# Eighteen small products ahead of the first scores, and part of the value loads asked for later

## The chip, the cores and the metric

One core of one Trainium2 chip. The metric is the device time of one execution in microseconds; the median over several executions is compared. Engines are named TensorE (matmuls, PE in the rows, with PEld for its weight loads), VectorE (DVE), ScalarE (ACT), GpSimd (POOL) and SyncE (SP), which issues nearly all transfers.

## What is computed

Strided attention, then a gated product with two matrices behind it, then a mixture of four experts. Everything is float32 in and out.

```python
# attention: batch 2, 8 heads, 576 positions, head size 64
scores = q @ k.T / 8                      # per head
mask_local   = (rel >= 0) & (rel < 32)    # heads 0 to 3
mask_strided = (rel >= 0) & (pos_k % 32 == pos_q % 32)   # heads 4 to 7
attn = softmax(where(mask, scores, -1e9)) # sum + 1e-9 in the denominator
x = (attn @ v)                            # to 1152 tokens x 512
# gated product
h = ((x @ w1) * (x @ w2)) @ w3            # 512 -> 1024 -> 1024
x = h @ w_out                             # 1024 -> 512
# experts
p = domain_probs / (sum(domain_probs) + 1e-9)
out = sum over e of p[:, e] * (relu(x @ w1[e]) @ w2[e])
```

## The kernel before

The order of all instructions is written out by hand, under one schedule from line 823 on; each engine does its instructions in that order. Four stages follow each other: attention of the first batch (lines 824 to 973), the first products of the weights w1 and w2 with the first batch's x, into which the second batch's attention is woven (974 to 1029), the small product of w3 and w_out (1030 to 1053), and the experts (1055 to 1126).

**Attention.** `warm_up` (107) makes a zeroed tile `idle` and sends products of it through TensorE that nobody reads; `keep_warm(n, parts)` sends n more of them, 128 columns for each part. One float32 product of this program appears in the trace as two weight loads and two matmuls. The batch has six chunks (`Chunk4`): three for the local heads (g = 0) and three for the strided heads (g = 1). A chunk goes through `masks` and `scores` (TensorE), `maxima` and `subtract` (VectorE), `exps` (ScalarE), the reciprocal of the sums (`sums`, or `slots_exps` and `recip` for chunk 1, VectorE), `normalise` (GpSimd, chunk 5 VectorE), `transposes` (TensorE), `evac` (ScalarE), `pv`, the product with the values (TensorE, line 483 for local and 492 for strided heads), and `put`, which stores the result in `x_whole` (ScalarE, line 521).

**Loads.** SyncE issues its transfers in program order, and the kernel's transfers rotate through eight semaphores. The values of the local heads come by `load_v_loc(b, c, behind)`, one load or three to a chunk; with `behind` given, GpSimd first copies a column of that tile into the target (328), so the transfer cannot be issued before the tile is written. `load_v_str` and `load_v_rest` bring the values of the strided heads, 54 = T3 partitions to a piece. In the kernel before, line 917 holds the second chunk's load behind the first chunk's maxima, and the third chunk's, the strided values and the rest follow it directly.

**Weights.** w1, w2, w_out and w3 arrive as 64-bit floats in chunks of 1 MB and are turned into float32 by integer steps: `round_up` (or `whole_low`) and `magnitude` on ScalarE, `clamp`, `shift`, `sign` and `add` (or `whole_steps`) on VectorE. Then each is split into a high part (`split_hi`, ScalarE) and a low part (`split_lo`, VectorE), and a product is three products, high by high, high by low and low by high (`mm3`, 301). The first chunk (`zero`, c_w12[0]) comes in two halves by `whole_load` (941) behind a GpSimd memset, is not split, and is multiplied with `x_whole` by `whole_product` (585) at lines 974 to 1002. The second (`one`) follows at lines 983 to 1007. From the third (`two`, c_w12[2]) on the steps run in the generator `work` (258), one step for each `advance`. At most two raw chunks wait in `rawp`, apart from three that borrow another place.

**Around the change**, TensorE's order is: warm-up, masks and scores 0, 1, 2, `keep_warm`, scores 3, transposes 0, scores 4, transposes 1, scores 5, pv 0, transposes 2, pv 1, transposes 3, pv 2, pv 3, transposes 4, `keep_warm(1, 2)`, transposes 5, pv 4, pv 5, then the whole products.

Of the kernel before, what the change touches and what calls it, by code (L numbers as in the profile page):

```python
# [8 lines left out]
F32 = mybir.dt.float32  # L9
# [5 lines left out]
ALU = mybir.AluOpType  # L15
# [3 lines left out]
P = 128  # L19
W = 32  # L20
# [4 lines left out]
T3 = 3 * NB  # L25
# [3 lines left out]
NBLK = NT // BLK  # L29
NTT = NT // P  # L30
NEG = -8.0e9
WARM = 2
SCALE = 1.0 / float(D) ** 0.5

EXP_LO, EXP_HI = 3.0517578125e-05, 122880.0
# [7 lines left out]
def kernel(  # L43
# [63 lines left out]
    def warm_up():  # L107

        idle = tmp.tile([P, P], F32, tag="pT", name="idle")
        nc.vector.memset(idle, 0.0)  # L110
        nc.scalar.activation(small.tile([P, 1], F32, tag="rec", name="one"), idle[:, :1], AF.Exp)
        moving = idle.unsqueeze(1).to_broadcast([P, 4, P])

        def keep_warm(n, parts=4):
            if n:
                acc = bank("idle").rearrange("p (a b) -> p a b", a=4)[:, :parts]
            for i in range(n):
                mm(acc, idle, moving[:, :parts], start=i == 0, stop=i == n - 1)

        keep_warm(WARM)  # L120
        return keep_warm


# [4 lines left out]
    class Chunk:  # L128
# [78 lines left out]
        def add_halves(self):  # L207
# [3 lines left out]
            for i in range(2):  # L211
                c = slice(512 * i, 512 * i + 512)
                self.add_half(i)
                nc.scalar.copy(self.hi[:, c], self.f32[:, c])

        def low_halves(self):
            for c in (slice(0, 512), slice(512, 1024)):
                nc.vector.tensor_tensor(out=self.lo[:, c], in0=self.f32[:, c], in1=self.hi[:, c].bitcast(F32),
                                        op=ALU.subtract)
            self.done = True  # L220

        def split_half(self, i, src):
            if i == 0:
# [26 lines left out]
    def load_next(held=False):  # L250
        nonlocal loaded
        if loaded < len(stream):
            stream[loaded].raw_load(held)
            loaded += 1
            for load in rest_loads.pop(loaded, ()):
                load()

    def work():


        wide = stream[2:20]
        before = None
        for c, after in zip(wide, wide[1:] + [None]):
            if before:
                while live > 14:
                    yield False
                before.split_hi()
            c.clamp()
            yield True
            if before:  # L270
                before.split_lo()
            c.shift()
            yield True
            c.sign()
            yield True
            if after:
                after.round_up()
                after.magnitude()
            c.add()
            yield True  # L280
            before = c
        while live > 14:
            yield False
        before.split_hi()
        yield True
        before.split_lo()
        yield True
        for w in c_e:
            yield from w.work()
# [11 lines left out]
    def mm3(acc, lhs, rhs, first, last):  # L301
        (lh, ll), (rh, rl) = lhs, rhs
        mm(acc, lh, rh, start=first, stop=False)  # L303
        mm(acc, lh, rl, start=False, stop=False)  # L304
        mm(acc, ll, rh, start=False, stop=last)  # L305


    x_hi = xp.tile([P, 4, NT], F32R, tag="x_hi", name="x_hi")
    x_lo = xp.tile([P, 4, NT], F32R, tag="x_lo", name="x_lo")
# [36 lines left out]
    def load_v_str(b):  # L346

        tv = big[0].tile([P, 12, P], F32, tag="big", name="tv_str")
        row = 5 * P
        for k in range(2):  # L350
            at = v_str[b, k, 0, 0]
            rows = bass.AP(tensor=at.tensor, offset=at.offset, ap=[[row, T3], [T3 * row, 2], [1, row]])
            nc.sync.dma_start(out=tv[64 * k:64 * k + T3, :10].rearrange("p (h t) d -> p h (t d)", h=2), in_=rows)
        vals[b, 1] = tv

    def load_v_rest(b):
        for k in range(2):
            nc.sync.dma_start(out=vals[b, 1][64 * k:64 * k + NB, 10:], in_=v_str[b, k, 2 * T3:2 * T3 + NB, :2])

    class Chunk4:  # L360
# [104 lines left out]
        def evac(self, copy):  # L465
            n = self.frames * P
            self.pT = tmp.tile([P, 512], F32, tag="pT", name="pT")[:, :n]
            copy(self.pT, self.tp)
# [81 lines left out]
    def ab_block(b, ft, n):  # L550
# [16 lines left out]
            hi, lo = (x[b, pair][:, ft % 2, n * HB:n * HB + HB] for x in (ab_hi, ab_lo))  # L567
        for w in range(2):
            acc = bank("ab_acc")[:, :HB]
            for k in range(4):  # L570
                mm3(acc, c_w12[ft].parts((w * 4 + k) * P, P), (x_hi[:, k, t], x_lo[:, k, t]), k == 0, k == 3)
            if w == 0:
                nc.scalar.copy(ab, acc)  # L573
            else:
                nc.vector.tensor_tensor(out=full, in0=acc, in1=ab, op=ALU.mult)
            yield
# [246 lines left out]
    with tc.manual_schedule():  # L823
# [91 lines left out]
        first[1].scores()  # L915
        first[0].maxima()
        load_v_loc(0, 1, first[0].mx[:, :1])
        load_v_loc(0, 2)
        load_v_str(0)
        load_v_rest(0)  # L920
        first[0].subtract()
        first[0].exps()
        first[2].scores()
# [7 lines left out]
        first[4].scores()  # L931
        exp_of(2)
        first[1].recip()
        first[1].normalise()
        evac(0)
        first[1].transposes()
        first[5].scores()
# [20 lines left out]
        scale_of(5)  # L958
        load_qk(1, 0, held=True)
        load_next()  # L960
        zero.whole_low(0)
        put(2)
        first[4].transposes()
        evac(4)
        zero.whole_low(1)
        keep_warm(1, 2)
        first[5].transposes()
        zero.whole_steps(0)
        first[4].pv()
        evac(5)  # L970
        put(3)
        put(4)
        first[5].pv()
        firsts = [ps_sc.tile([P, 512], F32, tag="sc", name="ab_acc")[:, :HB], bank("ab_acc")[:, :HB]]
# [214 lines left out]
```

## Time and profile before

| | us |
|---|---|
| median of 3 runs | 618.88 (617.59 to 619.91) |
| the profiled execution | 622.39 |
| its span, first to last instruction | 620.6 |
| TensorE busy | 611.4 (99%) |
| VectorE busy | 442.4 (71%) |
| ScalarE busy | 279.6 (45%) |
| GpSimd busy | 9.1 (1%) |
| mean granted clock of TensorE | 0.994 |

Times in the rows are counted from the first instruction of the span. Busy shares are means over the whole span, and the stages differ: attention of the first batch fills about the first 28 us. A matmul's end is modelled, so TensorE counts as busy while matmuls overlap; that it stood is read from the idle time in brackets and from the chain.

### The profile page before, as it was taken

What the parts mean: (1) busy time and instruction counts of PE and PEld (TensorE: products, weight loads), DVE (VectorE), ACT (ScalarE), POOL (GpSimd) and SP (SyncE); (2) the same over time, 40 slices, a digit from 0 to 9 for tenths busy, and PEclk for the clock granted to TensorE, in tenths of its full rate; (3) what the DMA queues carried; (4) which work ended last, traced back from release to release, by engine and by line L of the source; (5) the groups of instructions that cost most, each with busy time, mean ns of one, the idle gap of its engine ahead of it and who ended that gap; (6) DMA issues with size and microseconds to landing.
All of it is one profiled execution on the core that took longest, in us unless ns stands there. A gap on an engine that the chain in (4) does not pass through costs nothing.

```text
span 620.6 us, 11293 instructions
## 1 busy us (share of the span) xinstructions
PE 611.4 (99%) x4584; PEld 558.0 (90%) x4584; DVE 442.4 (71%) x796; ACT 279.6 (45%) x555; POOL 9.1 (1%) x33
## 2 busy tenths in 40 slices
PE   8799999999999999999999999999999999999998
PEld 5689999998889999999889999899989898989997
DVE  4699996988774126777876987888776665755843
ACT  4678974666643224433443334343433333333320
POOL 4100000000000000000000000000000000000000
PEclk9799999999999999999999999999999999999999
DMA  8967251244532111343354353445586556465411
GB/s 254 350 241 224 72 173 45 69 135 143 203 131 85 53 69 32 132 176 137 137 202 149 129 199 137 158 181 170 187 314 229 197 211 227 181 219 189 142 62 69
DMA packets 28403, 99.44 MB, mean 160 GB/s; under 512 B 2632, under 2 KB 6288, under 8 KB 25920
## 3 DMA queue, kind: packets, MB, share of 16 engines
q1 hardware_dynamic: 28080, 98.43, 45.1%
q8 instruction: 36, 0.59, 0.4%
q10 hardware_dynamic: 272, 0.29, 0.1%
q14 instruction: 15, 0.12, 0.1%
HBM read 79.58 MB, written 19.14 MB: 159 GB/s over the span
## 4 chain that ended last, share of the span: by engine, by line
PE 86%; DVE 5%; ACT 3%; DMA 3%; issue 2%; SPq 0%; DVEq 0%
PE g_acc L303 11%; PE g_acc L304 11%; PE g_acc L305 11%; PE m_a L305 4%; PE m_a L304 4%; PE m_a L303 4%; PE m_b L304 3%; PE m_c L303 3%; PE x_acc L305 3%; PE x_acc L303 3%; PE x_acc L304 3%; PE m_c L304 3%; PE m_b L303 3%; PE m_c L305 3%; PE m_b L305 3%; PE wc_acc L303 2%
## 5 line engine op out<-in xcount | busy, mean ns | idle before, releaser
L732 ACT ACTIVATE h_hi<-u 128x320 fp32r<-128x320 f32 (+1 forms) x128 | 56.9, 445 | 189.2 <-DVE u L738 189.2
L303 PE MATMUL g_acc<-w_hi,h_hi 128*128 128x512 f32 (+1 forms) x296 | 114.3, 386 | 0.0
L304 PE MATMUL g_acc<-w_lo,h_hi 128*128 128x512 f32 (+1 forms) x296 | 114.2, 386 | 0.0
L305 PE MATMUL g_acc<-w_hi,h_lo 128*128 128x512 f32 (+1 forms) x296 | 113.7, 384 | 0.0
L671 DVE TENSOR_TENSOR w_lo<-raw,w_hi 128x768 fp32r<-128x768 f32 x64 | 69.4, 1085 | 12.5 <-ACT w_hi L669 12.4
L738 DVE TENSOR_TENSOR u<-m_b,u 128x320 f32<-128x320 f32 (+1 forms) x96 | 40.8, 452 | 50.8 <-PE m_b L305 50.8
L303 PE MATMUL ab_acc<-x_hi,w_hi 128*128 128x288 f32 x240 | 71.7, 299 | 0.4 <-ACT ab L573 0.3
L304 PE MATMUL ab_acc<-x_lo,w_hi 128*128 128x288 f32 x240 | 70.7, 294 | 0.0
L305 PE MATMUL ab_acc<-x_hi,w_lo 128*128 128x288 f32 x240 | 70.7, 294 | 0.0
L305 PEld LDWEIGHTS g_acc<-w_hi,h_lo 128*128 128x128 f32 x296 | 55.6, 188 | 11.6
L303 PEld LDWEIGHTS g_acc<-w_hi,h_hi 128*128 128x128 f32 x296 | 55.8, 188 | 8.0
L304 PEld LDWEIGHTS g_acc<-w_lo,h_hi 128*128 128x128 f32 x296 | 55.7, 188 | 7.6
L734 DVE SCALAR_TENSOR_TENSOR h_lo<-u,h_hi 128x320 fp32r<-128x320 f32 (+1 forms) x128 | 57.7, 451 | 3.7 <-ACT h_hi L732 1.9
L669 ACT CAST w_hi<-raw 128x768 fp32r<-128x768 f32 x64 | 60.0, 937 | 0.0
L303 PEld LDWEIGHTS ab_acc<-x_hi,w_hi 128*128 128x128 f32 x240 | 45.0, 188 | 1.0 <-ACT ab L573 0.5
L304 PEld LDWEIGHTS ab_acc<-x_lo,w_hi 128*128 128x128 f32 x240 | 45.0, 188 | 0.0
L305 PEld LDWEIGHTS ab_acc<-x_hi,w_lo 128*128 128x128 f32 x240 | 45.0, 188 | 0.0
L304 PE MATMUL m_b<-b_t,s_hi 128*128 128x320 f32 (+1 forms) x128 | 37.9, 296 | 0.0
L738 DVE TENSOR_TENSOR u<-m_a,u 128x320 f32<-128x320 f32 (+1 forms) x64 | 28.9, 452 | 11.6 <-PE m_a L305 11.6
L671 DVE TENSOR_TENSOR s_lo<-raw,s_hi 128x1024 fp32r<-128x1024 f32 x16 | 19.6, 1226 | 24.3 <-ACT s_hi L669 24.3
L738 DVE TENSOR_TENSOR u<-m_c,u 128x320 f32<-128x320 f32 (+1 forms) x64 | 29.0, 453 | 4.5 <-PE m_c L305 3.9
L748 ACT COPY u<-m_a 128x320 f32<-128x320 f32 (+1 forms) x32 | 12.8, 400 | 42.1 <-PE m_a L305 42.1
(178 smaller groups left out, 1416.7 us busy)
## 6 DMA issues: line engine op xcount, KB each, us to landing
raw<-in_e_dram SPq DMA_DIRECT2D x32, 1024.0 KB, 5.2
raw<-in_w3T_dram SPq DMA_DIRECT2D x8, 1024.0 KB, 5.0
stored<-s_hi SPq DMA_DIRECT2D x16, 512.0 KB, 2.6
stored<-s_lo SPq DMA_DIRECT2D x16, 512.0 KB, 2.7
s_hi<-stored SPq DMA_DIRECT2D x16, 512.0 KB, 4.7
s_lo<-stored SPq DMA_DIRECT2D x16, 512.0 KB, 5.6
raw<-in_w_dram SPq DMA_DIRECT2D x7, 1024.0 KB, 6.5
raw<-in_w_out_dram SPq DMA_DIRECT2D x4, 1024.0 KB, 4.9
```

Source lines behind the costliest of these rows:

```text
L303: mm(acc, lh, rh, start=first, stop=False)
L304: mm(acc, lh, rl, start=False, stop=False)
L305: mm(acc, ll, rh, start=False, stop=last)
L669: nc.scalar.copy(dst[0], src)
L671: nc.vector.tensor_tensor(out=dst[1], in0=src, in1=dst[0].bitcast(F32), op=ALU.subtract)
L732: nc.scalar.activation(hi, src, AF.Relu)
L734: nc.vector.scalar_tensor_tensor(out=lo, in0=src, scalar=0.0, in1=hi.bitcast(F32), op0=ALU.max, op1=ALU.subtract)
L738: nc.vector.tensor_tensor(out=out, in0=acc, in1=b, op=ALU.add)
L748: nc.scalar.copy(u1, a)
```

## The change

The warm-up's second product of 512 columns becomes one of 256, and ahead of it come 18 products of a 64 x 64 piece of the zeroed tile with 32 columns. The third chunk's local values are held behind chunk 1's reciprocal, the strided values and the rest come behind chunk 1's `normalise` in program order, and the strided values are read for 64 partitions instead of 54. On ScalarE `put(2)` now stands ahead of `whole_low(0)`, and `whole_low(1)` between `put(3)` and `put(4)`. The third weight chunk is added and split by halves in `work`, and its first product runs all products with the high weights ahead of those with the low ones.

```diff
-        keep_warm(WARM)
+        keep_warm(1)
+        acc = bank("idle")
+        for i in range(FILL):
+            r = slice(64 * (i % 2), 64 * (i % 2) + 64)
+            mm(acc[r, :W], idle[r, :64], idle[r, :W], start=True, stop=True)
+        keep_warm(1, 2)
...
+        def low_half(self, i):
+            c = slice(512 * i, 512 * i + 512)
+            nc.vector.tensor_tensor(out=self.lo[:, c], in0=self.f32[:, c], in1=self.hi[:, c].bitcast(F32),
+                                    op=ALU.subtract)
+            self.done = i == 1
...
-            if before:
+            first_wide = before is wide[0]
+            if before and not first_wide:
                 while live > 14:
                     yield False
                 before.split_hi()
+            if first_wide:
+                before.low_half(0)
             c.clamp()
             yield True
-            if before:
+            if first_wide:
+                before.low_half(1)
+            elif before:
                 before.split_lo()
...
-            c.add()
+            if c is wide[0]:
+                while live > 14:
+                    yield False
+                c.add_halves()
+                load_next()
+            else:
+                c.add()
...
+    def high_first(acc, pairs):
+        for i, ((lh, _), (rh, rl)) in enumerate(pairs):
+            mm(acc, lh, rh, start=i == 0, stop=False)
+            mm(acc, lh, rl, start=False, stop=False)
+        for i, ((_, ll), (rh, _)) in enumerate(pairs):
+            mm(acc, ll, rh, start=False, stop=i == len(pairs) - 1)
...
-            rows = bass.AP(tensor=at.tensor, offset=at.offset, ap=[[row, T3], [T3 * row, 2], [1, row]])
-            nc.sync.dma_start(out=tv[64 * k:64 * k + T3, :10].rearrange("p (h t) d -> p h (t d)", h=2), in_=rows)
+            rows = bass.AP(tensor=at.tensor, offset=at.offset, ap=[[row, 64], [T3 * row, 2], [1, row]])
+            nc.sync.dma_start(out=tv[64 * k:64 * k + 64, :10].rearrange("p (h t) d -> p h (t d)", h=2), in_=rows)
...
+            if (b, ft, n, w) == (0, 2, 0, 0):
+                high_first(acc, [(c_w12[ft].parts((w * 4 + k) * P, P), (x_hi[:, k, t], x_lo[:, k, t]))
+                                 for k in range(4)])
...
         load_v_loc(0, 1, first[0].mx[:, :1])
-        load_v_loc(0, 2)
-        load_v_str(0)
-        load_v_rest(0)
...
         first[1].recip()
+        load_v_loc(0, 2, first[1].rec[:, :1])
         first[1].normalise()
+        load_v_str(0)
+        load_v_rest(0)
...
+        put(2)
         zero.whole_low(0)
-        put(2)
         first[4].transposes()
         evac(4)
-        zero.whole_low(1)
...
         put(3)
+        zero.whole_low(1)
         put(4)
```

FILL is 18.

## Rows read from the trace of the kernel before

**Rows 1.** The page, parts 1 and 3: busy us (share) xinstructions; queue, packets, MB

```profile
PE 611.4 (99%) x4584; PEld 558.0 (90%) x4584; DVE 442.4 (71%) x796; ACT 279.6 (45%) x555; POOL 9.1 (1%) x33
...
q8 instruction: 36, 0.59, 0.4%
```

**Rows 2.** Waits of TensorE, whole span: us in total, times, longest us

```profile
PE o L483 <- issue: 3.2, 1, 3.2
...
PE sc L401 <- DMA tqk<-in_qT_dram: 0.8, 1, 0.8
```

**Rows 3.** The chain in order of time, first 75 us: start us, us, what

```profile
16.83 3.17 issue
...
26.86 0.21 issue
...
28.10 7.97 PE ab_acc L588 x32
36.09 0.46 DVE ab_f L1002
```

**Rows 4.** Windows, 20.00 to 25.86: busy us, PEclk, DMA share, GB/s

```profile
20.00:25.86 5.86, 5.86 (x103) 5.07 (x103) 4.09 (x9) 2.96 (x8) 0.00 (x0) 0.50 0.98 376
```

**Rows 5.** Timeline of TensorE, to 24 us: start, us, operation, count [idle before]

```profile
1.05 3.78 PE L118 MATMUL idle<-idle 128*128 128x512 f32 x4 [1.05 <-DVE idle L110]
...
10.71 1.01 PE L410 MATMUL sc<-tqk 64*54 64x54 f32 x32 [0.23 <-DMA tqk<-in_qT_dram]
...
12.31 1.16 PE L410 MATMUL sc<-tqk 64*54 64x54 f32 x32
...
14.78 0.86 PE L483 MATMUL o<-pT,tv_loc 64*64 64x32 f32 x46
...
16.05 0.77 PE L483 MATMUL o<-pT,tv_loc 64*64 64x32 f32 x36
...
21.61 1.51 PE L483 MATMUL o<-pT,tv_loc 64*64 64x32 f32 x48
```

**Rows 6.** Windows, 19.90 to 26.95, between the two stops: instructions per engine in brackets

```profile
19.90:26.95 7.05, 6.87 (x125) 5.78 (x124) 5.04 (x10) 3.90 (x9) 0.00 (x0) 0.58 1.02 388
```

**Rows 7.** Instruction packets: transfer view of 10.3-10.4, 17.0-17.2, 24.6-24.9 (share of 16 engines)

```profile
q8 instruction: 1, 0.02, 69.6%
...
q8 instruction: 1, 0.02, 41.6%
...
q8 instruction: 1, 0.02, 21.2%
```

**Rows 8.** Timeline of SyncE's queue, 3 to 22 us: issue start, us, transfer, count

```profile
3.25 6.42 SPq L331 DMA_DIRECT2D tv_loc<-in_v_loc_dram  x7
10.59 1.29 SPq L353 DMA_DIRECT2D tv_str<-in_v_str_dram  x2
...
14.94 0.84 SPq L158 DMA_DIRECT2D raw<-in_w_dram  x2
18.84 0.33 SPq L138 DMA_DIRECT2D raw<-in_w_dram  x1
```

**Rows 9.** Timeline of VectorE, 11 to 36 us

```profile
11.21 0.19 DVE L454 RECIPROCAL rec<-rec 128x6 f32<-128x6 f32 x1
...
21.42 0.43 DVE L169 TENSOR_SCALAR w_whole<-raw 128x512 int32<-128x512 int32 x1 [2.18 <-DMA raw<-in_w_dram]
...
34.21 0.46 DVE L1002 TENSOR_TENSOR ab_f<-ab_acc,ab 128x288 f32<-128x288 f32 x1 [0.30 <-issue]
```

**Rows 10.** Timeline of GpSimd: the copy that holds back the second chunk's load

```profile
7.14 0.18 POOL L328 COPY tv_loc<-mx 128x1 f32<-128x1 f32 x1 [1.79 <-DVE mx L416]
```

**Rows 11.** Windows, 15 to 16 us, strided values alone in flight: DMA share, GB/s last

```profile
15.00:16.00 1.00, 1.00 (x48) 0.84 (x41) 0.96 (x4) 0.86 (x3) 0.00 (x0) 1.00 0.60 165
```

**Rows 12.** Timeline of ScalarE, 25 to 30 us

```profile
25.63 0.70 ACT L163 ACTIVATE raw<-raw 128x512 int32<-128x512 uint32 x1
...
28.89 1.16 ACT L147 ACTIVATE t<-raw 128x1024 f32<-128x1024 f32 x1
```

More of the change, by code (lines that the diff above doesn't have):

```diff
@@ L31 @@
 NEG = -8.0e9
-WARM = 2
+FILL = 18
 SCALE = 1.0 / float(D) ** 0.5
@@ L214, in add_halves @@
                 nc.scalar.copy(self.hi[:, c], self.f32[:, c])
+        def low_half(self, i):
[3 more added lines that the diff above has]
+            self.done = i == 1
         def low_halves(self):
[L217 to L220, printed above, removed]
+            for i in range(2):
+                self.low_half(i)
         def split_half(self, i, src):
@@ L569, in ab_block @@
             acc = bank("ab_acc")[:, :HB]
-            for k in range(4):
-                mm3(acc, c_w12[ft].parts((w * 4 + k) * P, P), (x_hi[:, k, t], x_lo[:, k, t]), k == 0, k == 3)
+            if (b, ft, n, w) == (0, 2, 0, 0):
+                high_first(acc, [(c_w12[ft].parts((w * 4 + k) * P, P), (x_hi[:, k, t], x_lo[:, k, t]))
+                                 for k in range(4)])
+            else:
+                for k in range(4):
+                    mm3(acc, c_w12[ft].parts((w * 4 + k) * P, P), (x_hi[:, k, t], x_lo[:, k, t]), k == 0, k == 3)
             if w == 0:
```

## The prediction

> **What bounds the kernel now.** I read the page first: TensorE is busy 99% of the span [rows 1], so the end can only move if work is taken from TensorE or if its dense stretch begins sooner. The view of waits then names one wait worth having: 3.2 us in front of a values product, put down to "issue", that is, to nothing that another engine or a transfer did [rows 2]. The chain in order of time shows where it lies and what follows: TensorE runs from one product to the next until 16.83, stands 3.17 us, stands again for 0.21 us at 26.86, and begins the first whole products of the weights (L588) at 28.10; at 36.09 the chain enters VectorE, whose steps and ScalarE's carry it on through the next stage [rows 3]. So what can be won lies before 28.10, and it arrives at the end only if VectorE and ScalarE, too, start their part of the chain sooner. The stop costs more than its 3.17 us: from 20.00 to 25.86 the granted clock is 0.50 (1.2 GHz instead of 2.4) [rows 4]. What that level costs is read from the same kind of product: 46 values products take 0.86 us before the stop and 48 take 1.51 us behind it [rows 5], a factor of 1.7; the 5.86 us of that stretch hold about 3.4 us of work at the full clock, so about 2.4 us went to the clock.
>
> **What the stop is.** It falls inside one group of 48 products that read the same two tiles, 36 before it and 12 behind it, so no late tile explains it. Queue 8 carries instructions: 36 packets and 0.59 MB, 16 KB each, for 4584 matmuls and 4584 weight loads, 255 instructions to a packet [rows 1]. Between the 3.17 us stop and the 0.21 us stop lie 125 matmuls and 124 weight loads, one packet's worth [rows 6]. The packets are seen at 10.3, 17.0 and 24.6; their shares times window times 16 engines give 1.11, 1.33 and 1.02 us of transfer [rows 7]. The ends are then near 11.5, 18.4 and 25.7, and TensorE goes on 1.4 to 1.6 us after the last two. The first fits as well: one packet's worth of instructions ahead of the big stop lies inside the 32 score products from 12.31, which take 1.16 us where the same group before took 1.01 [rows 5]; 13.1 is 1.6 us behind 11.5. So TensorE runs out of loaded instructions three times: by 0.1, 3.17 and 0.21 us. A request can be made at the latest when the block before it is entered, and the third packet started 4.6 us after TensorE entered that block at 20.00. Before 20.00 SyncE had issued a 1 MB weight chunk, at 18.84 [rows 8]. I read that as a queue: an instruction packet waits until the data asked for earlier has gone through its engine.
>
> The Trainium skill speaks against this twice. Its page "DMA: Bandwidth & Descriptors", section "Queues, rings and completion order", says that a DMA engine takes turns between its queues packet by packet, so a backlog of data should hardly delay an instruction packet; the 4.6 us above differ from that, and by the rule the sum would be that of rival B below. The Trainium skill's page "Runtime: NRT & Kernel Launch", section "Instruction fetch mechanics", calls the cost of a new instruction block mostly hidden; the 3.2 us of [rows 2] are not, and by that sentence the 72 instructions would be mere cost, rival D.
>
> **The 72 instructions.** 18 small products are 36 weight loads and 36 matmuls. The warm-up now has four matmuls of 512 columns in 3.78 us, 0.95 each [rows 5]; it gets two of 512 (1.89), two of 256 (0.95 by columns) and 36 small ones. Those cost 0.86/46 each at the full clock and 1.51/48 at the half, so 0.67 to 1.13 us; the engine is at the lower level there, and I take 1.1. Sum 3.9 against 3.78, 0.1 to 0.2 us later. It is hidden: the second scores wait 0.8 us for the queries [rows 2]. Without that cover it would cost those 0.2 us. Their effect is that each end of a block moves 36 pairs towards the front of the kernel's own work. The three stops move from the scores at 13.1 to the last pairs of the scores before (near 11.5), from 16.83 to the first product of that group (16.05), and from 26.86 to about three quarters through the fourth chunk's values products.
>
> **The loads.** Third local values, strided values and the rest are today the last of the loads asked for from 3.25 to 9.67 and those from 10.59 on [rows 8]; they go behind the second softmax's reciprocal, at 11.21 plus 0.19 [rows 9]. GpSimd's copy that holds them takes 0.18 [rows 10], so the three local loads go out from about 11.7. Seven local loads fill 6.42 us with waits between; I take 0.6 us of issue for each, so 13.5; the strided pair takes 1.29 and the rest about as long as its half, so SyncE is free at 15.5. GpSimd's own queue holds the second normalisation behind the copy: 0.1 to 0.2 us, hidden, because TensorE turns that chunk only after the fifth scores. Behind these loads on SyncE stands the first whole weight chunk, now asked for at 14.94 [rows 8] behind a GpSimd memset that follows the third normalisation; it goes out at the later of 15.5 and that memset.
> The strided load goes from 54 to 64 partitions. Where it runs alone the transfer engines are 0.60 busy at 165 GB/s [rows 11]; 9 of 16 is 0.56. 54 divides into 9 shares and 64 into 16, and I read the row so. Loads of 128 partitions fill the engines (1.02 in [rows 6]). The sum takes the same for 64: 0.55 MB at 165 is 3.3 us now; 0.65 MB at that rate over 0.60 is 2.4, so it wins about 0.9 us. If the spread stays as it is, the first chunk lands 0.9 us later and the VectorE steps, not TensorE, set the start.
>
> **The sum, fetch by fetch.** First block: asked for before the second scores, behind the same queries, keys and first local values; so I keep the start of before, 10.3. End 11.4, usable 12.9; needed at 11.45. A stop of 1.45 us (0 if the queue does not matter, 1.75 if it comes as late as before). The third group's maxima, and with them the softmax steps and the first weight chunk's memset, shift by as much, from 14.94 to 16.4. Second block: asked for at 12.9, behind two of the three local loads, so its packet starts near 14.2, ends 15.3, usable 16.9; needed at 16.05 plus 1.45. No stop. Third block: asked for at 16.9, behind the first half of the weight chunk or both; packet at 18.5 to 20.0, usable 21.1 to 22.6, middle 21.9. TensorE wants it at about 20.3: 1.6 us, half of the stop of before. I assume that the clock stays up. From that place, 36 pairs ahead of the stop at 26.86 and so near 23.5, TensorE now needs 4.6 us to 28.10, 2.4 of them at the half clock and 0.21 of them the stop: 2.4/1.7 + 2.0 = 3.4. The whole products begin at 25.3 instead of 28.10, 2.8 us sooner.
> ScalarE gains less: the second half's conversion (0.70) now stands behind the fourth chunk's stores, in front of the 1 MB chunk's magnitude at 28.89 [rows 12]. With the evacuations moving 2.7 us and 0.7 more in front, that step moves 2.0. VectorE, which follows, stands 0.3 us shortly before 36.09 [rows 9], so 36.09 moves by 2.0 to 2.8; I take 2.4. That chain then keeps its length: splitting the third weight chunk by halves starts ScalarE 0.6 us sooner but costs one more instruction on each engine, and the high-first order lets TensorE begin before the low half is there; the waits of TensorE name none for that chunk [rows 2], so I put it at 0, between -0.3 and +0.2. The swap of store and conversion is in the sum. 622.39 for the profiled execution (span 620.6 and 1.8 around it) becomes 620.0; the median of 618.88 lies 3.5 us under that execution, and I take the same 2.4 us off it: **616.5**. In timed executions the clock may fall less, which would make the gain smaller.
>
> **The rivals.** A: the stop is as long as before and only moves, and the clock falls again. Then the 2.4 us of clock cost stay and the gain is 0 to 0.8: about 618.5. For it: the third packet still stands behind a weight chunk. Against it: half of the queue in front of the second packet is gone. B: every block comes in time, because the queue is short or the packets do not wait. Then the first weight chunk sets the start. VectorE began its half 2.18 us after its last work, when the chunk landed at 21.42 [rows 9]; landing 1.5 to 2 us sooner and 2.9 us of steps give 23.0 to 23.5, and with ScalarE's 0.7 the gain is 3.5 to 5: about 614.6. C, slower: the first block comes later than today, behind the second local load as well, usable at 14.4. That is a stop of 3 us in the middle of the scores, about as long as the one that halved the clock, so the 5.4 us of small products from 11.45 to 16.83 run at the factor of 1.7: 3 + 3.8 = 6.8 us late against the 3.17 + 2.4 of before, and the third block adds 1.6 to 2: about +3, 622. It decides from a stop of about 3 us at the first boundary. D: the stop is no fetch at all; then the change costs its 0.2 us and 619 is the result.
>
> **How the numbers follow.** Forecast 0.40, A 0.13, B 0.33, C 0.07, D 0.07. The measurement can tell about 0.5%, 3.1 us, from no change, so faster means under 615.8 and slower over 622.0. B lies nearly all under 615.8, of the forecast about a seventh: faster 0.38. C lies half over 622.0: slower 0.04. The rest, 0.58, is within. Range: from 613.0, B's better part, to 619.3, D and A; outside are C and the best of B.
>
> **What would show it.** In the profile after: three stops put down to "issue", near 11.5, none near 16, one in the fourth chunk's products near 20; granted clock 1.00 from 20 to 26; whole products from 25.3; transfer engines over 0.9 busy while the strided values load; the chain entering VectorE near 33.7. If a stop of 3 us stands anywhere with 0.50 behind it, A or C is right; if no "issue" row is over 0.5 us, B; if the stop stays after 36 of those 48 products, D. Wrong altogether would be a new wait after 36 us that takes the gain back.

## The result: 1.1% slower

The changed kernel takes 625.32 us (median of 6, 624.64 to 625.57) where the kernel before takes 618.41 beside it (617.20 to 620.79): a ratio of 1.0106, interval 1.0084 to 1.0127. The profiled execution is 625.24 us with a span of 623.3; before it was 622.39 with 620.6. So the two profiles differ by 2.9 us and the medians by 6.9. What goes with the times is the mean granted clock, which is on record for the executions of the changed kernel and of all experiments: of 29 of the kernel before, timed beside four of the experiments, 15 have 0.999 or 1.000 and take 616.9 to 618.9 us, and 14 have 0.989 to 0.997 and take 619.2 to 625.7. (Over all experiments it is 61 of 124.) The profile of [rows 1 to 12] has 0.994, and all six of the changed kernel have 0.991 to 0.994.

### The profile page after: what moved, and what is told of

It reads as the page before. It is cut to its first block, busy times and chain, and to the rows that moved or that the text cites. A ratio compares the mean times of both kernels' runs of the same rounds, so it can differ in the third digit from the quotient of the medians.

```text
span 623.3 us, 11371 instructions
## 1 busy us (share of the span) xinstructions
PE 614.8 (99%) x4620; PEld 561.1 (90%) x4620; DVE 442.1 (71%) x798; ACT 279.5 (45%) x556; POOL 9.2 (1%) x34
## 4 chain that ended last, share of the span: by engine, by line
PE 91%; DVE 3%; ACT 3%; DMA 2%; issue 1%; SPq 0%; POOL 0%; DVEq 0%
PE g_acc L323 11%; PE g_acc L324 11%; PE g_acc L325 11%; PE m_a L325 4%; PE m_a L324 4%; PE m_a L323 4%; PE ab_acc L323 4%; PE ab_acc L325 3%; PE ab_acc L324 3%; PE m_b L324 3%; PE m_c L323 3%; PE x_acc L325 3%; PE x_acc L323 3%; PE x_acc L324 3%; PE m_b L323 3%; PE m_c L324 3%
## 5 line engine op out<-in xcount | busy, mean ns | idle before, releaser
L323 PE MATMUL ab_acc<-x_hi,w_hi 128*128 128x288 f32 x236 | 70.4, 298 | 1.0 <-ACT ab L604 0.9
```

## The profile after

The page, parts 1 and 3 (busy us, share, instructions; queue, packets, MB), as [rows 1]:

```profile
PE 614.8 (99%) x4620; PEld 561.1 (90%) x4620; DVE 442.1 (71%) x798; ACT 279.5 (45%) x556; POOL 9.2 (1%) x34
...
q8 instruction: 36, 0.59, 0.4%
```

36 more matmuls and weight loads, as said. The waits of TensorE, where [rows 2] had 3.2 us of "issue":

```profile
PE o L519 <- DMA tv_str<-in_v_str_dram: 2.2, 1, 2.2
...
PE ab_acc L323 <- ACT ab L604: 0.9, 1, 0.9
PE o L519 <- ACT x_whole L548: 0.4, 1, 0.4
PE tp L490 <- POOL p_ring L448: 0.4, 1, 0.4
```

No "issue" is left; a transfer is waited for instead, that of the strided values. The 0.9 us for ScalarE lie behind 120 us, where the kernel before waits 0.3 us for the same. The chain in order of time (start, us, what; lines are those of the changed kernel, 27 to 31 higher from the masks on), as [rows 3]:

```profile
3.12 2.06 PE idle L124 x36
...
7.30 1.22 PE sc L428 x48
8.54 0.57 DVE mx L443
...
11.15 0.19 DVE rec L481
11.34 0.44 DVE mx L443
11.88 0.57 DVE p_ring L451
12.47 0.53 ACT p_ring L457
13.01 0.19 POOL tv_loc L355
13.22 0.61 SPq L358
...
15.20 0.60 SPq L380
15.85 6.39 DMA tv_str<-in_v_str_dram
...
22.37 1.10 PE o L519 x28
...
28.26 9.79 PE ab_acc L619 x32
```

It runs without a gap from the small products through the first chunks' scores and softmax, GpSimd's copy and SyncE's issues to the landing of the strided values. In the timeline of SyncE's queue, as [rows 8], these loads and all behind them go out late:

```profile
9.37 5.79 SPq L358 DMA_DIRECT2D tv_loc<-in_v_loc_dram  x4
15.20 1.25 SPq L380 DMA_DIRECT2D tv_str<-in_v_str_dram  x2
16.50 0.90 SPq L385 DMA_DIRECT2D tv_str<-in_v_str_dram  x2
17.49 0.84 SPq L163 DMA_DIRECT2D raw<-in_w_dram  x2
```

The strided values are asked for at 15.20 instead of 10.59, the first weight chunk at 17.49 instead of 14.94. Windows (start:end, length, busy us of the engines, granted clock, DMA share, GB/s):

```profile
12.00:13.00 1.00, 1.00 (x22) 0.76 (x16) 0.92 (x4) 0.96 (x5) 0.32 (x1) 1.00 0.02 6
13.00:14.00 1.00, 1.00 (x33) 0.88 (x32) 0.97 (x3) 0.48 (x1) 0.99 (x3) 1.00 0.05 16
...
17.00:18.00 1.00, 0.64 (x43) 0.53 (x36) 0.96 (x3) 0.50 (x2) 0.96 (x2) 1.00 1.06 259
...
21.69:31.93 10.24, 9.56 (x110) 7.73 (x111) 6.67 (x13) 6.43 (x16) 0.00 (x0) 0.50 1.03 409
```

From 12 to 14 the transfer engines have next to nothing to do; once the strided values move, they are 1.06 busy (from 17.49 on with the first weight chunk), where [rows 11] had 0.60. From 21.69, while TensorE still stands for the values, the granted clock is 0.50, 1.2 GHz, for 10.2 us, where [rows 4] had 5.9: the first whole products run through it and take 9.79 us instead of the 7.97 of [rows 3].

The blocks of instructions themselves come in time in this profile. Their packets are seen in the transfer views of 9.6 to 9.8, 13.2 to 13.4 and 18.0 to 18.2. The third block is about this window:

```profile
16.68:22.86 6.18, 3.22 (x125) 2.74 (x125) 3.41 (x8) 2.79 (x10) 1.94 (x5) 0.91 1.04 284
```

It keeps TensorE busy for 3.2 of 6.2 us, and for 2.2 us TensorE stands in it for the values. Without that wait it would have wanted the next block near 20.7: in e2 and e7 the block ends behind 26 of these 32 products, so 22 of it, of 24 ns each in e8, are left at 20.14. The packet seen at 18.1 takes 1.3 us, and TensorE went on 1.2 to 1.6 us behind the end of others, so that the block could be used between 20.7 and 21.1. By this estimate a stop of at most 0.4 us lay behind the wait.

The end of those whole products carries nearly all of the time. It is the x32 row of the chain, start plus length:

| profiled kernel | whole products | span | difference |
|---|---|---|---|
| before | 28.10 + 7.97 = 36.07 | 620.6 | 584.5 |
| after | 28.26 + 9.79 = 38.05 | 623.3 | 585.3 |
| e8 | 28.48 + 9.68 = 38.16 | 623.4 | 585.2 |
| e9 | 24.00 + 7.97 = 31.97 | 616.0 | 584.0 |
| e11 | 24.81 + 7.97 = 32.78 | 617.0 | 584.2 |
| e14 | 26.46 + 7.97 = 34.43 | 619.0 | 584.6 |

So everything behind is the same to 1.3 us, and a span of 616 to 617 is one whose whole products end between 32 and 33.

## The experiments

Where the expectations use letters: W says that the small products cost, L that the moved loads do, S that only both together do, F that moved ends of instruction blocks bring new stops. Ratios are against the kernel before on the same chip.

### Each part alone

All of the change but the small products (e1), the small products alone (e2), the moved loads alone (e3), and the order of stores, halves and products alone (e4).

```diff
 e1: the changed kernel with
-        keep_warm(1)
-        acc = bank("idle")
-        for i in range(FILL):
...
+        keep_warm(WARM)
 e2: the kernel before with the lines that e1 takes out
 e3: the kernel before with
-        load_v_loc(0, 2)
-        load_v_str(0)
-        load_v_rest(0)
...
+        load_v_loc(0, 2, first[1].rec[:, :1])
         first[1].normalise()
+        load_v_str(0)
+        load_v_rest(0)
 e4: the kernel before with, among the rest
+        put(2)
         zero.whole_low(0)
-        put(2)
```

> The changed kernel with the warm-up of the kernel before: no small products. Theory W (the warm-up costs it): the first scores begin at 5.6 us again instead of 7.2, the two held loads follow 1.6 to 2 us sooner, the strided values land near 20.4 instead of 22.2; time 618 to 620. Theory L (the later loads cost it): the strided values still land late, TensorE still stands 2 us or more for them and the granted clock still falls; time 623 to 625. Theory S (the two delays only hurt together): the stop stays under 1 us, no fall of the clock behind it, 616 to 618.5. Instruction stops at the old places, 13.1 and 16.8, can come back in any of them.

> The kernel before with the small products in the warm-up alone. Theory W: first scores at 7.2, all the attention 1.6 us later or more; time 622 to 625. Theory L: the loads go out early, so the delay is hidden by them or by the instruction stop that goes away; 617 to 619. Theory S: 618.5 to 621, TensorE free of a long stop.

> The kernel before with the third local chunk, the strided values and the rest asked for behind the second reciprocal, still 54 partitions. Theory W: near the time of before, 617 to 620. Theory L: the strided values land past 21 us, TensorE stands for them, the clock falls; 622 to 625. Theory S: 618 to 620, a stop under 1 us.

> The kernel before with what is left of the change: the order of store and conversion on ScalarE, the third weight chunk by halves, the high weights first. All three theories: no difference that can be told, 618.0 to 618.8. If it were slower by over 2 us, part of the loss would lie behind 28 us and none of the theories would hold alone.

Measured: e1 621.64 (1.0048, interval 1.0029 to 1.0068), e2 622.20 (1.0064, 1.0038 to 1.0091), e3 621.40 (1.0037, 1.0015 to 1.0059), e4 620.50 (1.0017, 0.9988 to 1.0047). Waits of TensorE in e3, then in e2:

```profile
PE o L492 <- DMA tv_str<-in_v_str_dram: 3.1, 2, 2.6
```

```profile
PE o L497 <- issue: 1.2, 1, 1.2
```

The loads alone bring the wait for the strided values and no other of size. The small products alone bring a stop of "issue", now among the strided values products. Both cost by themselves: S falls, W and L each hold in part. The order of stores and halves is not told from nothing.

The losses differ in their clock. In e2, 4 of 9 executions have a mean of 0.999 or 1.000 and still take 620.2 to 622.2 us, some 3 us more than such executions of the kernel before beside them (617.1 to 619.1). In e1 and in e3 none of the 10 has. The chains of e1 (64 partitions) and e3 (54), where the strided values are asked for from 13.50 and 13.57, show their landing:

```profile
14.15 6.27 DMA tv_str<-in_v_str_dram
```

```profile
14.16 7.66 DMA tv_str<-in_v_str_dram
```

The spread is worth 1.4 us there, and e1 still waits 1.3 us for the values in all.

### The kernel before, profiled again

Unchanged, twice (the second is b2_before).

> The kernel before, unchanged, one more profiled execution: the first one took 622.4 us where 30 timed ones have a median of 618.3. Theory P (it was one of its slow executions): this one, if it is near 618, shows a stop for instructions under 3 us near 16.8 or less than the 6.8 us at a granted clock of 0.50 behind it, and the whole products begin 2 to 4 us sooner than 28.1. Theory Q (profiling itself adds the 3.5 us): it takes 622 again with the same stop and the same fall.

622.90 and 622.14 us, "issue" stops of 4.2 and 3.7 us: what was expected if profiling itself adds the time. With the profile of [rows 1 to 12] that makes three of three, while about half of the timed executions keep their clock. Profiling is no fixed cost, for the profiled executions of e9 and e14 have a mean of 0.999 and are among the three shortest of their twelve (617.78 and 620.78). Whether it makes the long stop likelier in this kernel was not settled. No execution of the kernel before that keeps its clock was profiled, so it is argued and not shown that the 3.5 us between the first profile and the median are the stop and its clock.

### The small products behind the first scores

The 18 small products stand behind the first chunk's scores, the warm-up is the old one; e6 with the loads as changed, e6b with the loads and 54 partitions of before.

```diff
         first[0].scores()
+        fill_acc, zeros = bank("idle"), keep_warm.zeros
+        for i in range(FILL):
+            r = slice(64 * (i % 2), 64 * (i % 2) + 64)
+            mm(fill_acc[r, :W], zeros[r, :64], zeros[r, :W], start=True, stop=True)
         first[1].scores()
```

> The changed kernel with the old warm-up and the 18 small products behind the first scores, where TensorE waits for the queries anyway: block ends stand where the change puts them, the first scores don't wait. Theory W2 (they cost by standing ahead of the first scores): 620 to 622, no worse than the changed kernel without them (621.6). Theory F (it is the moved block ends that cost): 624 to 626, with stops for instructions at new places.

> As e6_fill_late, but with the loads where the kernel before has them and 54 partitions again. Theory W2: no stop near 16.8, one of about 1 us in the fourth chunk's products, 616 to 619. Theory F: 621 to 624, as the small products alone cost it ahead of the first scores (622.2).

622.44 (1.0044, 1.0015 to 1.0073) and 623.34 (1.0055, 1.0025 to 1.0084). Waits of TensorE in e6:

```profile
PE o L516 <- issue: 1.8, 1, 1.8
PE sc L434 <- issue: 1.8, 1, 1.8
```

The two results point different ways. With the loads of before (e6b), the small products cost behind the first scores what they cost in the warm-up, 1.0055 beside e2's 1.0064: that speaks for F. With the moved loads (e6) they cost nothing that can be told: 1.0044 is where the kernel without them stands (e1, 1.0048), and it is well under the changed kernel's 1.0106, although two stops of "issue" come with them. That speaks for W2: in the changed kernel the small products cost by standing ahead of the first scores, about 0.6%.

### The strided values early again

The changed kernel, with only the third chunk's local values held back.

```diff
         load_v_loc(0, 1, first[0].mx[:, :1])
+        load_v_str(0)
+        load_v_rest(0)
...
         first[1].normalise()
-        load_v_str(0)
-        load_v_rest(0)
```

> The changed kernel, with the strided values and the rest asked for behind the first maxima again, as before the change; only the third chunk's local values stay behind the second reciprocal. Small products and 64 partitions stay. If the late landing of the strided values is what the moved loads cost, the stop of 2.2 us on them is gone here, they land near 17, and the time is that of the small products alone, 621.5 to 622.7. If the emptied queues cost by themselves, or the held third chunk does (its products then wait), it stays at 624 to 625.5.

624.40 (1.0079, 1.0048 to 1.0109): the wait for the strided values is gone and the time is not. In its place, among the same products:

```profile
PE o L519 <- issue: 2.3, 1, 2.3
```

This stop is not one that the changed kernel hid. There the third block is entered at 16.7, 0.8 us before the first weight chunk is asked for (17.49), and the next packet is seen at 18.1. In e7 the chunk goes out at 16.70, 1.0 us before the block is entered at 17.66, and the packet is seen in the transfer view of 21.0 to 21.2. So e7 exchanges the wait for the values for a block that comes late behind the chunk.

### The warm-up shortened to its old length

The kernel before with the small products and without the last 256-column product (e8); and the same with the first weight chunk asked for 4 us later (e13).

```diff
 e8: in the new warm-up
-        keep_warm(1, 2)
 e13: and also
-        zero.whole_load()
-        loaded = 1
         evac(1)
...
+        zero.whole_load()
+        loaded = 1
         load_next(True)
```

> The kernel before with one warm-up product pair, the 18 small products, and nothing of 256 columns behind them, so that the warm-up takes about 1.2 us less than with the whole new warm-up, and the first scores begin near 6.0 instead of 7.23 (5.58 before). If the small products cost by the start that they put off, the time is 0.4 to 1 us over the kernel before, 619 to 619.5 where that is 618.4. If they cost by the block ends that they move, it stays 3 to 4 us over it, 621.5 to 622.5, with an issue stop of over 1 us near 21. Should the clock rise later for want of the last products, the first scores are at the lower level and it lies between.

> The kernel with the 18 small products and the shorter warm-up, with the first whole weight chunk asked for some 4 us later (at about 20.4 instead of 16.5), right ahead of the second one. If a block of instructions waits behind data that was asked for before it, the packet that started at 21.05 there starts here at 16.5 to 18, and the stop of 2.4 us near 23.2 is gone; what comes instead is a late weight chunk, whole products 1 to 3 us later than there, and 625 to 627.5. If the packet's time has nothing to do with the data, it stays near 21 with the stop of 2.4 us.

e8 takes 625.01 us (1.0082, 1.0051 to 1.0112), though its first scores start at 6.19, 1.0 us sooner than in the changed kernel and 0.6 later than in the one before. TensorE's timeline of e8 (start, us, operation, count, idle before):

```profile
13.10 0.20 PE L414 MATMUL sc<-tqk 64*54 64x54 f32 x1 [1.25 <-issue]
...
17.48 0.90 PE L487 MATMUL o<-pT,tv_loc 64*64 64x32 f32 x48
...
20.19 0.68 PE L496 MATMUL o<-pT,tv_str 54*64 54x54 f32 x28
23.23 0.46 PE L496 MATMUL o<-pT,tv_str 54*64 54x54 f32 x4 [2.36 <-issue]
```

and windows of e8, then of e13:

```profile
17.49:20.66 3.17, 2.86 (x129) 2.47 (x128) 3.02 (x7) 2.12 (x7) 1.95 (x5) 1.00 0.88 301
...
18.00:19.00 1.00, 0.83 (x32) 0.69 (x24) 1.00 (x2) 0.47 (x2) 0.56 (x2) 1.00 0.91 315
...
22.00:23.00 1.00, 0.00 (x0) 0.00 (x0) 0.82 (x3) 0.00 (x0) 0.00 (x0) 0.50 0.88 307
```

```profile
17.64:20.80 3.16, 2.85 (x129) 2.46 (x128) 3.01 (x7) 2.12 (x7) 1.98 (x6) 1.00 0.02 6
...
18.00:19.00 1.00, 0.84 (x42) 0.73 (x35) 0.97 (x3) 0.47 (x2) 0.70 (x2) 1.00 0.06 16
```

The block of e8 from 17.5 holds 129 matmuls and 128 weight loads, one packet's worth, and is through in 3.17 us. In e13 the same block begins at 17.64 and takes 3.16 us. The packet with the next block is found in the transfer view of 21.0 to 21.2 in e8 and, after a stretch with the engines 0.06 busy instead of 0.91, in that of 18.9 to 19.1 in e13 (the line of the instruction queue, in this order):

```profile
q8 instruction: 1, 0.02, 30.6%
```

```profile
q8 instruction: 1, 0.02, 28.7%
```

In e13 TensorE reaches the same place with almost no stop, and waits later for ScalarE, which waits for the late chunk:

```profile
21.19 0.32 PE L496 MATMUL o<-pT,tv_str 54*64 54x54 f32 x4 [0.17 <-issue]
...
26.33 0.75 PE L496 MATMUL o<-pT,tv_str 54*64 54x54 f32 x32 [3.36 <-ACT pT L472]
```

625.97 us (1.0115, 1.0073 to 1.0157): time and stop are as expected, the packet is 1.0 us later than the latest expected, 18. So from entering this block to the next one's packet it is 3.5 us in e8 and 1.3 in e13: the data ahead of the packet is worth some 2.1 to 2.2 us of it, and 1.3 remain with idle transfer engines.

### The delay without the block ends, and half of the block ends

A warm-up of 6 products of 512 columns and no small ones (e11); 9 small products (e10).

```diff
 e11: the kernel before with
-WARM = 2
+WARM = 3
 e10: the new warm-up with
-FILL = 18
+FILL = 9
```

> The kernel before with a warm-up of 6 products of 512 columns instead of 4: it lasts about as long as the new one (first scores near 6.5 to 7.2), but moves the block ends by two pairs only. If the later start is what costs, the time is 1 to 2 us over the kernel before, 619.5 to 620.5. If the moved block ends cost, it is within 0.7 us of the kernel before, 618 to 619, because the wait for the first fetched block at 13.1 takes up the delay.

> The kernel before with 9 small products instead of 18 in the new warm-up, so the warm-up is about 1 us shorter than with 18 and the block ends move by 18 pairs instead of 36. If the small products cost by the block ends that they move, the third end in the kernel's own work lies 18 pairs later than with 18 of them, still ahead of the fourth chunk's last products, and the cost is about the same as that of 18, 620.5 to 622.5 against 618.4. If they cost by their time, it is half or less of that, 619 to 620.

e11: 618.16 beside 618.91 (0.9978, 0.9951 to 1.0005). Its timeline and a window of it:

```profile
1.05 5.49 PE L118 MATMUL idle<-idle 128*128 128x512 f32 x6 [1.05 <-DVE idle L110]
...
6.95 2.21 PE L401 MATMUL sc<-tqk 64*32 64x64 f32 x144
...
10.76 1.01 PE L410 MATMUL sc<-tqk 64*54 64x54 f32 x32
...
17.83 0.43 PE L483 MATMUL o<-pT,tv_loc 64*64 64x32 f32 x14 [0.98 <-issue]
```

```profile
17.82:23.54 5.72, 5.71 (x124) 4.77 (x125) 4.71 (x12) 3.73 (x10) 0.98 (x3) 0.70 0.97 345
```

The first scores start 1.4 us later than in the kernel before, at 6.95 instead of 5.58, but the strided scores at 10.76 where [rows 5] have 10.71: the waits for queries there, 0.8 and 0.2 us, are not in e11, and nothing is lost at the end. The block of the same number as in e8's window takes 5.72 us here: with its end 32 pairs further back it takes in the transposes and empty products that follow, part of it runs at the lower clock behind the 0.98 us stop (mean 0.70), and no stop comes behind it. e10 gives 620.57 (1.0021, 0.9988 to 1.0055), not told from the kernel before; its executions at a clock of 1.000 take 618.4 to 619.9 and its others up to 623.5. With that interval it decides neither way.

### Work added to the short block

e8 with two empty products of 512 columns in the block that ran in 3.17 us (e14); e11 with one in the block that stops in the kernel before (e15).

```diff
 e14
         evac(3)
+        keep_warm(2)
         first[3].pv()
 e15
         first[2].transposes()
+        keep_warm(1)
         first[1].pv()
```

> The kernel with the 18 small products and the shorter warm-up (625.01), and two more empty products of 512 columns ahead of the fourth chunk's values products, 1.6 us of TensorE at the full clock, inside the block of 256 instructions that ran in 3.2 us there and ended in the 2.4 us stop. If the loss is that this block is shorter in time than the fetch of the next, the added work fills the stop: it shrinks to under 1.2 us, the granted clock stays at 1.00 past 22, the whole products begin before 27.5 instead of 28.4, and the time falls to 621.5 to 624 although work was added. If the small products cost by themselves, the stop moves and the time is 625 to 627.

> The kernel with the longer warm-up and no small products (618.16), and one more empty product of 512 columns, 0.8 us, in the block that ended there in a stop of 0.98 us. By the same theory the stop shrinks to 0.2 us or nothing, and the time is 617 to 618.3, with more of the executions at a mean granted clock of 1.00; at most 0.5% under the kernel before. If the stop is not a matter of the block's length in time, the added product costs its 0.8 us: 618.5 to 619.5.

e14: 621.38 us (1.0045, 1.0020 to 1.0070), 3.6 us under e8's 625.01 with 1.9 us of work added. Timeline and windows of e14:

```profile
19.90 1.98 PE L118 MATMUL idle<-idle 128*128 128x512 f32 x4
...
22.95 0.34 PE L496 MATMUL o<-pT,tv_str 54*64 54x54 f32 x8 [0.57 <-issue]
```

```profile
17.60:22.20 4.60, 4.55 (x126) 3.06 (x125) 4.38 (x10) 2.79 (x8) 1.59 (x5) 1.00 0.83 256
...
22.00:24.00 2.00, 1.43 (x38) 1.22 (x34) 1.82 (x4) 0.04 (x1) 0.00 (x0) 1.00 0.98 401
```

The block takes 4.6 us, the stop is 0.6 instead of 2.4, and the clock stays at 1.00; 8 of 12 executions have a mean of 0.999 or 1.000, of e8's six none. So the short block and the clock behind it are the cause of about half of e8's loss: 6.7 us over the kernel before beside it became 3.3 (the intervals of the two ratios still overlap a little). In the 3.3 us are the 1.9 of added work; the executions of e14 that keep the clock take 620.5 to 621.8, those of the kernel before beside them 617.1 to 618.0. e15 came out the other way: 619.18 (1.0003, 0.9975 to 1.0031), what was expected if the length of the block does not matter, and its stop is still 1.53 us in the profiled execution. Filling that block is no gain. Its packet is seen at 16.6 to 16.8, e11's at 15.4 to 15.6; why it came late was not settled.

### The spread alone

The kernel before with the strided values over 64 partitions (e5); the same with them ahead of the third local ones (e9); the same with only the third local ones held (e12).

```diff
 e5
-[[row, T3], [T3 * row, 2], [1, row]]
+[[row, 64], [T3 * row, 2], [1, row]]
 e9: and also
+        load_v_str(0)
         load_v_loc(0, 2)
-        load_v_str(0)
 e12: e5, and
-        load_v_loc(0, 2)
...
+        load_v_loc(0, 2, first[1].rec[:, :1])
```

> The kernel before with the strided values spread over 64 partitions and nothing else. If the spread is worth what the prediction took for it (0.9 us of landing), the transfer engines stand near 1.05 instead of 0.60 while these values load, the raw halves of the first weight chunk land about 1 us sooner, and the time is 617.5 to 618.5 against 618.4. If it is worth nothing at the end because the products then wait for instructions instead, there is no difference that can be measured.

> As the one with 64 partitions alone, and the strided values are asked for ahead of the third chunk's local ones instead of behind them: the reverse of what the change does. If an early landing of the strided values is worth something at the end, this is at or under the 64 partitions alone, 616.5 to 618; if they are never waited for in the kernel before, it is the same; if the third chunk's local values come late by it, there is a wait of 0.5 to 1.5 us on them and the time is 619 to 620.

> The kernel before with 64 partitions, and only the third chunk's local values held behind the second reciprocal; the strided values are asked for early; no small products. With less data ahead of the second block's instructions, their packet starts near 14.8 as with the same loads and the small products, so the stop before the second block is gone, and the third block's end lies in the fourth chunk's products. If the stops are a matter of what is queued when a block is asked for, the time is 617 to 618.5 and its spread is narrower than that of the kernel before. If holding a load costs by itself, it is 619.5 to 621.

e5 619.68 (1.0017, 0.9996 to 1.0039), e9 620.23 (1.0016, 0.9992 to 1.0040), e12 619.54 (1.0012, 0.9987 to 1.0036): no difference that can be told, and none of the gains expected. e12's packet is seen at 14.6 to 14.8, as expected, but the stop that should have gone with it is still 1.5 us, and a second one of 1.0 us follows. A window of e9 while the strided values and the third local ones load, and its timeline:

```profile
14.00:15.00 1.00, 1.00 (x55) 0.95 (x55) 0.90 (x3) 0.53 (x2) 0.39 (x3) 1.00 1.13 242
```

```profile
18.30 0.42 PE L483 MATMUL o<-pT,tv_loc 64*64 64x32 f32 x12 [1.52 <-issue]
```

The transfer engines are full, and TensorE waits for instructions instead. No version beats the kernel before measurably; e11 comes nearest.

## Why the prediction was wrong

**The stop and its cause: right.** Stops put down to "issue" come at the ends of blocks of about 256 instructions, and the packets wait behind data: e8 beside e13 shows 2.1 us of it. The Trainium skill's page "Runtime: NRT & Kernel Launch", section "Instruction fetch mechanics", calls the crossing of a block mostly hidden; here stops of up to 4.2 us (b1) are not. The page "DMA: Bandwidth & Descriptors" of the Trainium skill, section "Queues, rings and completion order", lets queues take turns by packet, so a backlog should delay little; e8 and e13 differ from that by the same 2.1 us. In the changed kernel all three blocks come in time, where the sum had stops of 1.45 and 1.6 us. "If no issue row is over 0.5 us, B" is met by that, but B let the first weight chunk set the start next, and it is the strided values that set it.

**The step that failed first: no price was put on the moved loads.** The prediction followed what stands behind them on SyncE (the weight chunk: 15.5 or 16.4 said, 17.49 measured) but not when the strided values themselves land. e1, without small products, asks for them at 13.50, just where the prediction had them, and with its spread; TensorE waits 1.3 us for them there, 2.2 in the changed kernel and, with 54 partitions, 3.1 in e3. The trace of the kernel before has the number: these transfers land 6.9 to 7.1 us after their issue. From 13.5 and 14.1, less the 0.9 us that the prediction gave the spread, that is 19.5 to 20.3, and it had TensorE three quarters through these products at 20.3: no margin was left. Emptied queues, 0.02 and 0.05 of the engines from 12 to 14, did bring the blocks in time, as meant: the gain and the loss are the same act.

**The second: "I assume that the clock stays up".** All six executions of the changed kernel have a mean of 0.991 to 0.994, and in the profile the clock is 0.50 for 10.2 us. Its price there is about 3.8 us, an estimate from rows at both levels: 1.8 in the whole products (9.79 against 7.97), 1.6 from the transposes ahead of them to their start (4.8 us, and 3.2 in e9 at 1.00), and 0.4 in the 28 products behind the wait (1.10, and 0.68 in e8 at 1.00). The whole products begin at 28.26 instead of 25.3 and end at 38.05.

**The third block: where it does come late, about right in place and size.** The prediction wanted that block at 20.3, in the fourth chunk's values products, and had 1.6 us of stop (with a range up to 2.3). e2 shows 1.2 there, e7 2.3, e8 2.4. Moving the block's end forward by 36 pairs did not spare a fetch; it left a block made of small products alone, 3.2 us long (5.7 in e11, part of it at the lower clock), and put its stop right ahead of the whole products: they take 9.68 us in e8, and the granted clock is 0.50 from 22 on. e14 fills that block, and half of e8's loss is gone. In the changed kernel the wait for the values stands in the same place.

**The small products: mis-sized.** 1.1 us was taken, 2.06 measured, 57 ns each where 31 was the dearer of the two prices read; the prediction took the engine to be at the lower level there, and the windows of the profile give a granted clock of 1.00. The net delay of the first scores is 1.65 us instead of 0.1 to 0.2. With the loads of before it matters little: e11 makes up 1.4 us by the waits for queries, and e8 takes 1.0 us of the delay away and is no faster. With the moved loads it counts, for the chain runs from the warm-up through the first softmax steps to these loads: the second reciprocal comes at 12.68 (before: 11.21, [rows 9]), GpSimd's copy behind it at 13.01, and the loads go out from 13.22 where 11.7 was said, and SyncE is free at 17.4 instead of 15.5. Of the wait of 2.2 us e1 has 1.3, and e6, without the delay, is at 1.0044 where the changed kernel is at 1.0106.

**The 2.4 us taken off the median.** The profile showed 2.4 us of clock and 3.2 of stop, and the prediction took a part of them off a median of 618.88. Executions of the kernel before at a full clock take 616.9 to 619.1 us, so at that median little of the clock's part was left to win. "In timed executions the clock may fall less" stood there as a remark; it should have been in the sum. The profiled execution is 5.2 us over the 620.0 forecast for it, the median 8.8 over 616.5: about 3.6 us of the miss are this base.

**The rivals.** C had the size of the difference between the profiles, about +3, by the wrong place: the first block came no later (its packet is seen at 9.7, before at 10.3) and no stop stands in the scores. A is nearest, a stop that only moves and takes the clock along, but here a transfer ends it, and its 618.5 has the same error in the base.

**The rest.** The spread over 16 engines instead of 9 fits the share, 0.60 to 1.06, and the 1.4 us between e1 and e3. The Trainium skill's page "DMA: Bandwidth & Descriptors", section "Why a DMA increments its semaphore by 16 and not by 1", gives the largest number up to 16 that divides the slowest dimension of both access patterns, which for 54 is 9 and for 64 is 16; the trace agrees, with 0.60 where 9 of 16 is 0.56. Behind the whole products only the wait for ScalarE has grown, to 0.9 us from 0.3, and the differences of the table hold to 1.3 us. Which part of the changed kernel's 6.9 us each cause has is not settled. Alone they are 3.9 (e2) and 3.1 (e3) by the medians, which happens to add up, but e2's stop for instructions is not in the changed kernel, and e7, which takes the wait for the values out of it, brings a late block in.

## What to carry to other kernels

A profile shows one kind of execution; before a stop in it is counted as something to win, the granted clock of the timed executions has to say that they have it as well. Where instructions are fetched in blocks, count what a block holds in time and not in instructions: a block of nothing but small matmuls can be over before the next is there, and empty work in it can be cheaper than the stop (it was in e14 and was not in e15). And a load that is moved back to make room is priced by when its own reader wants it, not only by what it lets through, with the time to landing that the trace already shows.

## What the runs showed that was not expected

Of one unchanged kernel half of the executions keep TensorE's clock and half do not, 616.9 to 625.7 us. The length of a stop alone does not tell which: in e9 the granted clock is 1.00 behind a stop of 1.52 us, in e5 it is 0.50 from 19 to 25 behind one of 0.97. A packet of instructions starts 1.3 us after the block ahead of it is entered even with the transfer engines at 0.06 (e13). Products of 64 by 64 by 32 take 57 ns each in the warm-up, where the windows of the profile give a granted clock of 1.00, and 31 ns each further on at 0.50 (1.51 us for 48, [rows 5]); what makes the first ones slow was not settled.
